# Attention, routed experts and a feed-forward layer on one core: drains on POOL, attention's tiles in two pools, weight conversions at other times

## The chip, the cores and the metric

The kernel runs on one core of a Trainium2 chip. The metric is device time in microseconds of one execution; it was 872.88 us in the median of three runs (872.65 to 874.85). One execution was also profiled. The core's engines work side by side, each through its own instructions in order: TensorE (PE), VectorE (DVE), ScalarE (ACT), GpSimd (POOL) and SyncE (SP, which here issues most DMAs).

## The reference

Three layers follow each other; all is float32 except the last layer's weights, which come as float64 (the kernel reads them as pairs of 32-bit words).

```python
# attention: batch 4, heads 8, sequence 576, head 64
scores = q @ k.T / sqrt(64);  cum = cumsum(maximum(s, 0))
scores = where(causal, -1e9, scores + minimum(-(cum[..., :, None] - cum[..., None, :]), 0))
x = softmax(scores) @ v                      # -> 2304 tokens of 512
# experts: 8 of 512 -> 1024 -> 512, one for each token
e_idx = argmax(x @ w_gate)
out[mask_e] = gate_w * eom_e * (maximum(x[mask_e] @ w1[e], 0) @ w2[e])
# feed-forward: 512 -> 2048 -> 512
y = square(maximum(out @ w_in, 0)) @ w_out
```

## The kernel before

Attention goes over 16 pairs of heads and ends near 224 us. Its tiles lie in a stack of pools that is closed after it; the pools of the later stages are then opened on the same addresses. The first of them, `stg`, holds three staging buffers of 4 KB a partition; `wpool2` with the weight slots w2 and w3 (32 KB each) follows.

The expert stage has 64 units. Unit n = 8 g + f handles slice f (128 hidden features) of expert g, for all tokens of that expert at once (352 token rows for the first, less for the later ones; the first 128 of expert 0 are computed earlier). Its work is H (`emit_h`, L1426, twelve matmuls of xt and w into PSUM), a split of the rectified result into a high and a low part (`emit_hv`: ACT writes the high part at L1436, DVE the low part at L1437), and Y (`emit_y`, L1468, twelve matmuls: the first eight read the high part, the last four the low part). The operands are float32r tiles, and each value is held as a high part and the rest; weights are split alike: `w_load` (L237) brings 512 KB into a staging buffer from SP's queue, `w_hi` (L246) writes the high part on ACT, `w_lo` (L250) the low part on DVE. Eight such jobs make an expert's weights.

The order on each engine is written by hand. `at(key, function)` files a piece of work under a key, counted in units; all pieces are emitted in the order of their keys, and where two keys are equal in the order of filing. An engine's queue is then worked through in that order: a piece that waits holds up what was filed behind it on the same engine. H of unit n has key n, its split n + 0.9, its Y n + 2.1, so Y runs behind H of two units later. The four PSUM sums of an expert are copied out by `emit_yv` on ACT (L1515, key 9.5 after the expert's start) and must be free before the next expert's first Y.

```python
at(n, emit_h, g, g, f, f)
at(n + K_['hv'], emit_hv, g, f)
at(n + 2.1, emit_y, g, g, f, f, NF)
```

Among these units sixteen pieces of the feed-forward weights are converted from float64 to float32 in DRAM, one in K_['cvp'] units from key K_['cv0'] on. A piece is loaded at K_['cvl'] = 2.5 units before its key (L1366; the first two from ACT's queue, the others from SP's), worked on by ACT (L1378, L1382) and DVE (L1376 to L1390), put together on POOL (`cv_c`, L1394 and L1395) in a single buffer cvm, and stored from ACT's queue (L1400, key + 2.4); the next piece's L1382 waits for that store to land. The other sixteen pieces are converted in the feed-forward stage.

Before unit 0, the first 128 tokens of expert 0 go through `early_h` (L1069) and `early_y` (L1097), which read hidden values from the tile `st_a[1]` of attention; `early_store` (key 0.5, L1584 to L1587) writes their result.

The feed-forward stage works on six tiles of 384 tokens; each tile's result is stored by `y_store` (L1536) with three indirect DMAs from POOL, which puts the rows at their tokens' places. After the last tile comes a loop for overflowing experts that runs zero times here, and the program's closing instructions, which the profile puts down to L1813.

Of the kernel before, what the change touches and what calls it, by code (L numbers as in the profile page):

```python
# [13 lines left out]
F32R = mybir.dt.float32r  # L14
# [10 lines left out]
P = 128  # L25
# [5 lines left out]
    S=3,  # L31
# [42 lines left out]
    exs=5.6,  # L74
    exl=8.6,
    cvm=0.7,
    cvp=3.5,
    cv0=4.0,
    cvl=2.5,
    ws=0.75,  # L80
    wh=0.3,
# [9 lines left out]
def attention_moe_ffn_kernel(  # L91
# [14 lines left out]
    nc = tc.nc  # L106
    B, H, S, D = q.shape
    NT, DM = out.shape
    E = w_gate.shape[1]
# [14 lines left out]
    NTILE = NT // TT  # L124
# [92 lines left out]
    def at(key, fn, *args):  # L217
        tasks.append((key, len(tasks), fn, args))
# [33 lines left out]
    def w_job(job, t_load, t_hi, t_lo):  # L252
        if job not in raw:
            at(t_load, w_load, job)
        at(t_hi, w_hi, job)
        at(t_lo, w_lo, job)
# [18 lines left out]
    def half_jobs(e, ab):  # L275
        return [((e, ab), i) for i in range(4)]
# [4 lines left out]
    def rows_of(g):  # L281
        if g >= E:
            return [P] * CT
        return [P] * (CAPS[g] // P) + ([CAPS[g] % P] if CAPS[g] % P else [])
# [4 lines left out]
    def cols_of(g):  # L289
        return sum(rows_of(g)) - P * first_of(g)  # L290
# [159 lines left out]

    with tc.manual_schedule():
        with ExitStack() as actx:
            apool = actx.enter_context(tc.tile_pool(name="apool", bufs=1))
            cq_p = actx.enter_context(tc.tile_pool(name="cq", bufs=1))
            qk_p = actx.enter_context(tc.tile_pool(name="qk", bufs=3))
# [9 lines left out]
            p2ctx = ExitStack()  # L465
            ps_2 = p2ctx.enter_context(tc.tile_pool(name="ps_2", bufs=1, space=PSUM, side="right"))

            st_a = [apool.tile([P, 4, S], F32R, name=f"sta{a}") for a in range(3)]
            st_b = [apool.tile([P, 4, S], F32R, name=f"stb{a}") for a in range(2)]

            def st_of(pp):
                return st_a[pp % 3], st_b[pp % 2]
# [873 lines left out]
        def x_trans(g, c, t, d=0.0):  # L1346
            at(t, x_pe, g, c)
            at(t + d + 0.001, x_hi, g, c)
            at(t + 2 * d + 0.002, x_lo, g, c)
# [177 lines left out]
        def y_store(g):  # L1527
            ysb = ysb_t.pop(g)
            if g < E:
                n = cols_of(g)  # L1530
                dst = yT_d.rearrange("(k p) n -> p k n", p=P)
                nc.sync.dma_start(
                    out=dst[:, :, P:P + n] if g == 0 else dst[:, :, ds(reg_o[g], n)], in_=ysb[:, :, 0:n])
                return
            for c in range(CT):
                put = nc.gpsimd.indirect_dma_start(  # L1536
                    out=out[:, :], out_offset=bass.IndirectOffsetOnAxis(ap=tok_m[:, (g - E) * CT + c, 0:1], axis=0),
                    in_=ysb.rearrange("p a n -> p (a n)")[:, c * DM:(c + 1) * DM], in_offset=None)
                nc.gpsimd.memset(gap, 0.0)
                for old in puts:  # L1540
                    tc.declare_no_dep(put.ins, old.ins, reason="the rows of two sorted chunks are different tokens")
                puts.append(put)

        def pos_tokens():
            w = gt2("pz", [B * NB, E])
            nc.vector.tensor_tensor(
                out=w, in0=oh_all.rearrange("p b t e -> p (b t) e"),
                in1=R["v"][:, 1:2].to_broadcast([P, B * NB, E]), op=ALU.mult)
            x = gt2("py", [B * NB])
            nc.vector.tensor_reduce(out=x.unsqueeze(2), in_=w, axis=AX.X, op=ALU.add)  # L1550
            nc.vector.tensor_tensor(
                out=pos_i.rearrange("p b t -> p (b t)"), in0=x, in1=rk_all.rearrange("p b t -> p (b t)"), op=ALU.add)
            nc.vector.tensor_copy(out=tok[:, :, :, 1].bitcast(F32), in_=gsq)
# [49 lines left out]
        for n in range(NS):  # L1603
            g, f = divmod(n, NF)
# [3 lines left out]
        for g in range(E):  # L1608
            n0 = g * NF
            if g:  # L1610
                at(n0 + NF + 1.0, load_regs, [g], 1, reg_o, NT)
            if g > 1:
                at(n0 - NF - 1.5, load_regs, [g], 0, reg_e, E - 1)
            at(n0 + NF + 1.5, emit_yv, g)
            at(n0 + NF + 1.8, y_store, g)
            if g + 1 < E:
                for c in range(len(rows_of(g + 1))):
                    x_trans(g + 1, c, n0 + K_['xt0'] + K_['xt1'] * c if g else 4.2 + 1.0 * c, 0.3)
            if g + 2 < E:
                at(n0 + (6.7 if g == 0 else 5.5), gather, g + 2)  # L1620
            hj = half_jobs(g + 1, "a") + half_jobs(g + 1, "b")
            at(n0 + 2.15, alloc_next)
            at(n0 + 2.15, alloc_next)
            for i, job in enumerate(hj):
                ta = n0 + 2.2 + i
                if g + 1 == E and i >= 6:
                    continue
                w_job(job, -0.7 if g == 0 and i < 4 else ta - K_["wld"], ta + K_['wh'], ta + K_['wl'])
# [34 lines left out]
        for v, (t, f0, f1) in enumerate(visits):  # L1663
            g = E + t
            if v > 1 and not (f0 and t not in spilled):
                n0 = n - 6 if v == 2 else n - 7.5
                at(n0 - 4.0, load_xf, t)
                for i in range(2):
                    ks = (i * KD // 2, (i + 1) * KD // 2)
                    at(n - 5.04 + 2 * i, xf_hi, t, *ks)  # L1670
                    at(n - 5.04 + 2 * i, xf_lo, t, *ks)
            for f in range(f0, f1):
                e = E + f // NF
                at(n, emit_h, g, e, f, f % NF)
                at(n + 0.9, emit_sq, g, f)
                at(n + 0.94, emit_hs, g, f)
                left = NTILE * NF2 - 1 - n
                if left == 0:
                    at(n + 2.1, emit_y_end, g, e, [f - 1, f], NF2)
                elif t in spilled:  # L1680
                    at(n + 2.1, emit_y, g, e, f, f % NF, f1, f0)
                elif left > 1:
                    at(n + 2.1, emit_y, g, e, f, f % NF, NF2)
                n += 1
            if f1 == NF and t in spilled:
                for c in range(CT):
                    at(n + 1.97 + c, emit_ym, g, c)
            elif f1 == NF2:
                at(n + 1.2, emit_ys if t in spilled else emit_yv, g)
                at(n + 1.8, y_store, g)  # L1690
# [15 lines left out]
        else:  # L1706
            for i, job in enumerate(half_jobs(E + 1, "a") + half_jobs(E + 1, "b")):
                ta = 3.5 + 3.0 * i
# [108 lines left out]
```

## Time and profile before

| | us |
|---|---|
| median of three runs | 872.88 |
| the runs | 872.65, 872.88, 874.85 |
| the profiled execution | 871.05 |
| its span, first to last instruction | 869.3 |
| PE, DVE, ACT, POOL busy in it | 843.5, 519.9, 452.1, 261.4 |

The stages of the profiled execution: attention until about 224 us, the early part of expert 0 until 238.7, the 64 units until about 459, the feed-forward layer until 856, and closing instructions until 869.3. PE's rows give the start of matmuls that run on into one another; their lengths overlap, so the time of a group of twelve is read from its start to the next group's start. In brackets stands the idle time of the engine just before a row, and what ended it. Rows of a queue ("ACTq", "SPq") are instructions of its sequencer, such as the issue of a DMA; they do not count as busy.

### The profile page before, as it was taken

The numbers are of one execution on the slowest core, as the hardware profiler recorded it, in microseconds if no ns is written. First come the engines' busy times: TensorE is split into PE (matmuls) and PEld (weight loads), VectorE is DVE, ScalarE is ACT, GpSimd is POOL, SyncE is SP. The second block draws the span as 40 slices with busy tenths as digits, with TensorE's granted clock in tenths as the row PEclk, the third lists the DMA queues.
The fourth block names the chain that finished last, engine by engine and source line by source line (L and its number), as shares of the span: only waits on it lengthen the run. The fifth ranks groups of instructions, "written<-read, shape, count | busy, mean of one in ns | idle before, by whom it ended". The sixth has DMA issues, their size and how long they took to land.

```text
span 869.3 us, 15155 instructions
## 1 busy us (share of the span) xinstructions
PE 843.5 (97%) x5412; PEld 748.8 (86%) x5412; DVE 519.9 (60%) x1186; ACT 452.1 (52%) x1008; POOL 261.4 (30%) x302
## 2 busy tenths in 40 slices
PE   7999999999999999999999999999999999999993
PEld 5876777777789999999999999999999999999992
DVE  8667777978768587668866667664333333232220
ACT  6687878988446556566555555443323232223221
POOL 4322234543136575566412233331101101001001
PEclk9999999999999999999999999999999999999998
DMA  6666677753178898899883442321010111001001
GB/s 155 147 157 145 142 181 179 176 130 94 42 268 250 271 266 244 241 272 284 291 241 98 134 135 84 109 85 49 37 37 37 59 51 37 1 1 37 1 1 39
DMA packets 113028, 113.14 MB, mean 130 GB/s; under 512 B 66033, under 2 KB 83953, under 8 KB 112946
## 3 DMA queue, kind: packets, MB, share of 16 engines
q1 hardware_dynamic: 106162, 96.97, 40.9%
q0 software_dynamic: 3664, 9.62, 3.2%
q10 hardware_dynamic: 3120, 5.51, 1.8%
q8 instruction: 45, 0.74, 0.4%
q14 instruction: 37, 0.30, 0.1%
HBM read 80.50 MB, written 23.32 MB: 119 GB/s over the span
## 4 chain that ended last, share of the span: by engine, by line
PE 52%; issue 30%; ACT 5%; DVE 4%; DMA 4%; POOL 3%; SPq 0%; POOLq 0%; ACTq 0%; DVEq 0%
PE z L1426 17%; PE z L1468 10%; PE z L1477 7%; PE t L731 5%; PE s L634 4%; PE t L694 4%; ACT p L678 2%; POOL out_dram L1536 2%; DMA w_out_d<-cvm 1%; DMA cv<-in_moe_w_in_dram 1%; ACT sta L574 1%; PE t L547 1%; ACT pt L713 1%; PE z L333 1%; PE s L769 1%
## 5 line engine op out<-in xcount | busy, mean ns | idle before, releaser
L1426 PE MATMUL z<-xt,w 128*128 128x384 f32 (+6 forms) x1920 | 329.9, 320 | 1.9 <-DVE h L1437 1.9
L1426 PEld LDWEIGHTS z<-xt,w 128*128 128x128 f32 x1920 | 308.3, 188 | 10.8 <-DVE h L1437 2.1
L1477 PE MATMUL z<-w,h 128*128 128x512 f32 x864 | 214.9, 393 | 0.0
L1477 PEld LDWEIGHTS z<-w,h 128*128 128x128 f32 x864 | 160.8, 188 | 29.3
L1446 DVE SCALAR_TENSOR_TENSOR r<-z,r 128x384 f32<-128x384 f32 x96 | 53.3, 555 | 129.1 <-ACT r L1445 127.5
L1445 ACT ACTIVATE r<-z 128x384 f32<-128x384 f32 x96 | 47.2, 491 | 153.5 <-PE z L1426 150.6
L1468 PE MATMUL z<-h,w 128*128 128x304 f32 (+5 forms) x768 | 112.1, 295 | 0.1
L1468 PEld LDWEIGHTS z<-h,w 128*128 128x128 f32 x768 | 105.3, 191 | 0.6 <-ACT ysb L1515 0.3
L1394 POOL TENSOR_TENSOR cvm<-cvm,cva 128x512 f32<-128x512 f32 x32 | 47.2, 1475 | 182.6 <-DVE cva L1390 135.5
L1536 POOL DMA_INDIRECT out_dram<-ysb,tok_m x18 | 17.4, 969 | 245.5 <-ACT ysb L1523 183.2
L1453 DVE TENSOR_TENSOR h<-r,h 128x384 fp32r<-128x384 f32 x96 | 60.9, 635 | 50.3 <-ACT h L1452 47.4
L678 ACT ACTIVATE p<-p,nm 128x128 f32<-128x128 f32 (+3 forms) x144 | 84.3, 590 | 4.8 <-DVE nm L661 4.7
L1452 ACT CAST h<-r 128x384 fp32r<-128x384 f32 x96 | 49.3, 513 | 63.6 <-DVE r L1446 63.2
L661 DVE CUSTOM_DVE_ANT_0 p<-s,mask 128x128 f32<-128x128 f32 (+3 forms) x128 | 59.5, 485 | 29.1 <-PE s L634 28.0
L694 PE MATMUL t<-ident,p 128*128 128x128 f32 x400 | 69.5, 283 | 2.6 <-DVE sta L578 1.1
L250 DVE TENSOR_TENSOR w<-stg,w 128x1024 fp32r<-128x1024 f32 x49 | 68.7, 1401 | 0.8 <-ACT w L246 0.8
L246 ACT CAST w<-stg 128x1024 fp32r<-128x1024 f32 x49 | 51.5, 1051 | 20.3 <-POOL cvm L1395 19.4
L694 PEld LDWEIGHTS t<-ident,p 128*128 128x128 f32 x400 | 44.4, 140 | 18.8 <-ACT p L678 6.8
L595 POOL CAST stb<-sta 64x1152 fp32r<-64x1152 f32 x28 | 31.4, 1150 | 79.3 <-PE s L634 47.7
L1395 POOL TENSOR_TENSOR cvm<-cvs,cvm 128x512 f32<-128x512 f32 x32 | 54.0, 1688 | 2.5
L634 PE MATMUL s<-sta 128*64 128x288 f32 (+4 forms) x204 | 50.1, 342 | 3.3 <-ACT sta L574 1.2
L1437 DVE SCALAR_TENSOR_TENSOR h<-z,h 128x304 fp32r<-128x304 f32 (+5 forms) x64 | 28.5, 445 | 40.8 <-ACT h L1436 33.9
(242 smaller groups left out, 1041.6 us busy)
## 6 DMA issues: line engine op xcount, KB each, us to landing
stg<-in_moe_w_dram SPq DMA_DIRECT2D x42, 512.0 KB
cv<-in_moe_w_out_dram SPq DMA_DIRECT2D x16, 512.0 KB
stx<-in_moe_w_dram SPq DMA_DIRECT2D x14, 512.0 KB
cv<-in_moe_w_in_dram SPq DMA_DIRECT2D x14, 512.0 KB
xr<-yT_d SPq DMA_DIRECT2D x8, 768.0 KB
qk<-in_q_dram SPq DMA_DIRECT2D x32, 128.0 KB
qk<-in_k_dram SPq DMA_DIRECT2D x32, 128.0 KB
v<-in_v_dram SPq DMA_DIRECT2D x32, 128.0 KB
```

The costliest lines, as they stand in the source:

```text
L246: nc.scalar.copy(out=w_parts(job)[0], in_=raw[job])
L250: nc.vector.tensor_tensor(out=lo, in0=raw.pop(job), in1=hi.bitcast(F32), op=ALU.subtract)
L634: nc.tensor.matmul(ps[0:mw, d0:d0 + nn], lhsT=ql[r, m0:m0 + mw], rhs=kl[r, c0:c0 + nn], start=(i == 0 and (tail or n == 0)), stop=(done an ...
L661: nc.vector.tensor_tensor_reduce(out=dst, in0=src, in1=msk, scale=-1.0, scalar=3.0e38, op0=ALU.add, op1=ALU.min, accum_out=nm[:, c:c + 1])
L678: nc.scalar.activation(out=pt[:, cs], in_=pt[:, cs], func=AF.Exp, scale=-1.0, bias=nm[:, c:c + 1], accum_out=rs[:, r:r + 1])
L694: nc.tensor.transpose(tp[:, i * P:(i + 1) * P], pt[:, j0:j0 + P], ident)
L1395: nc.gpsimd.tensor_tensor(out=m, in0=sq, in1=m, op=ALU.add)
L1426: nc.tensor.matmul(ps[:, 0:n], lhsT=wa[:, zw, kk, fl * P:(fl + 1) * P], rhs=xt[:, zx, kk, 0:n], start=(i == 0), stop=(i == 3 * KD - 1))
L1446: nc.vector.scalar_tensor_tensor(out=gg, in0=ps[:, 0:TT], scalar=0.0, in1=gg, op0=ALU.max, op1=ALU.mult)
L1453: nc.vector.tensor_tensor(out=ht[:, 1], in0=gg, in1=ht[:, 0].bitcast(F32), op=ALU.subtract)
L1468: nc.tensor.matmul(y_acc[g][d][:, 0:n], lhsT=wb[:, zw, fl, d * P:(d + 1) * P], rhs=ht[:, zh, 0:n], start=(f == 0 and i == 0), stop=(f == n ...
L1477: nc.tensor.matmul(acc, lhsT=ht[:, zh, c * P:(c + 1) * P], rhs=wb[:, zw, fl, :], start=(first and i == 0), stop=(last and i == 2))
```

## The change

Four things change. In the feed-forward stage a `drain` is put on POOL behind the stores of every tile but the last. Attention's tiles `st_a[0]` and `st_b[0]` come from a pool of their own that lies ahead of the pool with all others. Expert 1's weights are allocated from key 0.1 and converted with keys 0.2 + 1.2 i (high part + 0.3, low part + 0.7) in place of 2.2 + i; the loads of jobs 4 to 7 keep their lead of 2.9. The feed-forward weights are converted from key 6.0 on, one in 3.4 units, in place of 4.0 and 3.5.

```diff
-    cvp=3.5,
-    cv0=4.0,
+    cvp=3.4,
+    cv0=6.0,
...
+            apool0 = actx.enter_context(tc.tile_pool(name="apool0", bufs=1))
             apool = actx.enter_context(tc.tile_pool(name="apool", bufs=1))
...
-            st_a = [apool.tile([P, 4, S], F32R, name=f"sta{a}") for a in range(3)]
-            st_b = [apool.tile([P, 4, S], F32R, name=f"stb{a}") for a in range(2)]
+            st_a = [(apool if a else apool0).tile([P, 4, S], F32R, name=f"sta{a}") for a in range(3)]
+            st_b = [(apool if a else apool0).tile([P, 4, S], F32R, name=f"stb{a}") for a in range(2)]
...
                 puts.append(put)
+            if g + 1 < E + NTILE:
+                nc.gpsimd.drain()
...
-            at(n0 + 2.15, alloc_next)
-            at(n0 + 2.15, alloc_next)
+            at(n0 + 2.15 if g else 0.1, alloc_next)
+            at(n0 + 2.15 if g else 0.1, alloc_next)
             for i, job in enumerate(hj):
-                ta = n0 + 2.2 + i
+                ta = n0 + 2.2 + i if g else 0.2 + 1.2 * i
...
                 w_job(job, -0.7 if g == 0 and i < 4 else ta - K_["wld"], ta + K_['wh'], ta + K_['wl'])
```

## Rows read from the trace of the kernel before

**Rows 1.** The page, part 1: busy us (share of the span) xinstructions.
```profile
PE 843.5 (97%) x5412; PEld 748.8 (86%) x5412; DVE 519.9 (60%) x1186; ACT 452.1 (52%) x1008; POOL 261.4 (30%) x302
```

**Rows 2.** Windows: length, busy of PE, PEld, DVE, ACT, POOL, clock, DMA share, GB/s.
```profile
253.00:256.50 3.50, 1.62 (x15) 1.39 (x14) 3.36 (x6) 3.50 (x7) 1.63 (x2) 1.00 0.55 162
256.50:260.00 3.50, 3.50 (x18) 3.30 (x18) 3.36 (x10) 1.19 (x2) 1.79 (x1) 0.51 0.44 120
```

**Rows 3.** Timeline, PE: start, duration, engine, line, op, names, shape, [idle before, releaser].
```profile
243.15 1.50 PE L1468 MATMUL z<-h,w 128*128 128x224 f32 x12
244.49 1.50 PE L1426 MATMUL z<-xt,w 128*128 128x224 f32 x12
...
255.44 1.94 PE L1426 MATMUL z<-xt,w 128*128 128x224 f32 x12 [1.88 <-DVE h L1437]
257.18 2.76 PE L1468 MATMUL z<-h,w 128*128 128x224 f32 x12
259.87 0.47 PE L333 MATMUL z<-ident,xr 64*128 64x64 f32 x4
```

**Rows 4.** Timeline of ACT and its queue, 241 to 253 us.
```profile
241.77 0.36 ACT L1436 ACTIVATE h<-z 128x224 fp32r<-128x224 f32 x1 [0.51 <-ACT ysb L1586]
241.79 0.50 ACTq L1366 DMA_DIRECT2D cv<-in_moe_w_in_dram  x1
...
242.59 1.04 ACT L246 CAST w<-stg 128x1024 fp32r<-128x1024 f32 x1
...
252.04 0.69 ACT L1378 ACTIVATE cvs<-cv 128x512 f32<-128x512 f32 x1 [5.29 <-DMA cv<-in_moe_w_in_dram]
```

**Rows 5.** Timeline of DVE, 242 to 253 us.
```profile
242.16 0.39 DVE L1437 SCALAR_TENSOR_TENSOR h<-z,h 128x224 fp32r<-128x224 f32 x1 [1.71 <-ACT ysb L1586]
...
245.30 1.22 DVE L250 TENSOR_TENSOR w<-stg,w 128x1024 fp32r<-128x1024 f32 x1
...
252.04 0.43 DVE L1376 TENSOR_SCALAR cva<-cv 128x512 int32<-128x512 int32 x1 [3.03 <-DMA cv<-in_moe_w_in_dram]
```

**Rows 6.** Waits of SP's queue, 200 to 300 us: total, times, longest.
```profile
SPq L237 <- PE z L1097: 3.2, 1, 3.2
```

**Rows 7.** Timeline of SP's queue near 239 us.
```profile
239.02 1.46 SPq L237 DMA_DIRECT2D stg<-in_moe_w_dram  x3
```

**Rows 8.** Timeline of ACT and its queue, 427 to 440 us.
```profile
427.21 0.33 ACTq L1400 DMA_DIRECT2D w_out_d<-cvm  x1
...
433.25 0.69 ACT L1382 ACTIVATE cvm<-cv 128x512 f32<-128x512 uint16 x1 [1.15 <-DMA w_out_d<-cvm]
433.83 1.23 ACT L1515 COPY ysb<-z 128x272 f32<-128x272 f32 x4
...
439.28 0.33 ACTq L1400 DMA_DIRECT2D w_out_d<-cvm  x1
```

**Rows 9.** Timeline of PE, H of units 57, 58 and 59.
```profile
429.60 1.59 PE L1426 MATMUL z<-xt,w 128*128 128x256 f32 x12
...
432.54 1.58 PE L1426 MATMUL z<-xt,w 128*128 128x256 f32 x12
...
436.29 1.60 PE L1426 MATMUL z<-xt,w 128*128 128x256 f32 x12
```

**Rows 10.** Line L1813: durations in ns (min/median/max), first and last start.
```profile
L1813 POOLq DRAIN  x3: 51/103/5048, 863.4 to 869.0; - x3
```

**Rows 11.** Line L1802, the program's start, the same columns.
```profile
L1802 POOLq DRAIN  x1: 187/187/187, 0.4 to 0.4; - x1
```

**Rows 12.** Timeline of POOL, 852 to 870 us.
```profile
853.78 0.95 POOL L1536 DMA_INDIRECT out_dram<-ysb,tok_m  x1 [57.75 <-ACT ysb L1523]
```

**Rows 13.** DMA issues of POOL's queue, the three largest groups.
```profile
xr<-x_d,tbl_p POOLq DMA_INDIRECT x20
tok_d<-tok,pos_i POOLq DMA_INDIRECT x20
...
out_dram<-ysb,tok_m POOLq DMA_INDIRECT x18
```

## Prediction

> **What bounds the kernel now.** I began with the page's busy shares: TensorE's matmuls cover 97% of the span [rows 1], so only a stretch in which PE waits or runs at its low clock, or one in which nothing is computed, can give time back. I then read the windows and PE's timeline, looking for such stretches. There are three that this diff reaches.
>
> The first lies in unit 5 to 6 of the expert stage (a unit is one slice of 128 hidden features: twelve matmuls of L1426, H, and twelve of L1468, Y). An undisturbed group of twelve takes 244.49 - 243.15 = 1.34 us. Then PE idles for 1.88 us until DVE has finished a hidden slice (L1437), the next H takes 257.18 - 255.44 = 1.74 us and the next Y 259.87 - 257.18 = 2.69 us [rows 3]. The granted clock was 1.00 in the stretch that holds the idle time and 0.51 in the one after it, so the second loss is the 1.2 GHz level behind the first [rows 2]. Why the slice was late is seen on the in-order queues: the first load of FFN weights was issued from ACT at 241.79, and ACT (5.29 us) and DVE (3.03 us) both stood until 252.04 with that conversion at their heads [rows 4, 5]. Loss: 1.88 + 0.40 + 1.35 = 3.6 us.
>
> The second is small: H of unit 57 to H of unit 58 takes 432.54 - 429.60 = 2.94 us, the next one 436.29 - 432.54 = 3.75 us [rows 9], because ACT waited 1.15 us for a weight store to land before it could copy expert 6's sums out of PSUM (L1382 at 433.25, then L1515 at 433.83) [rows 8]. Loss: 0.8 us.
>
> The third is the tail. The last row stores start at 853.78 [rows 12], and among the closing instructions POOL has one DRAIN of 5.05 us, the first of its three, at 863.4 [rows 10]. It ends at 868.4, in a span of 869.3.
>
> **FFN conversion from unit 6 on.** The load moves from key 1.5 to 3.5, the conversion from 4.0 to 6.0, so the distance stays 2.5 units. Undisturbed that is 2.5 x 2 x 1.34 = 6.7 us, less than the 10.25 us that the load took now. What shortens it is what it competes with: at 241.79 it was issued right behind four loads of expert 1 that had left from 239.02 on [rows 7]; from key 3.5 it is issued after those have mostly landed. I place the issue at 245.6 and ACT's need for it at 254.5 (hidden slice 5 and two transposes stand ahead of it), 8.9 us apart. If the load still took 10.25 us, ACT would wait 1.3 us, a quarter of today's 5.29 us, and Y runs two units behind its slice, which hides that. So all 3.6 us go. The ends: 0 if the wait only moves, 3.6 if it goes.
>
> **Expert 1's conversion from unit 0.5.** Eight high parts on ACT (1.04 us each, row at 242.59) and eight low parts on DVE (1.22 us, row at 245.30) are the same work as before, spread over 1.2 units each and begun two units earlier. What is new is who stands behind the first. Its high part gets key 0.5 and goes ahead of hidden slice 0 on ACT, at about 241.77, where slice 0 starts now. Its low part gets key 0.2 + 0.7, which is 0.8999 in floating point, and so goes ahead of slice 0 (0.9) on DVE as well. Slice 0 is then ready on ACT at 241.77 + 1.04 + 0.36 = 243.17, just when PE wants it (243.15), but on DVE only at 242.85 + 1.22 + 0.39 = 244.46, in place of 242.16 + 0.39 = 242.55 [rows 3 to 5]. Y reads the high parts for its first eight matmuls and the low part from the ninth on, that is from 243.15 + 8 x 0.11 = 244.05. PE waits 0.4 us there. I take 0.4; the ends are 0 (Y only starts later in a queue that catches up) and 1.9, the longest PE wait in the trace [rows 3]. Later high parts stand at most one slice ahead of a hidden slice that Y needs two units later, which hides them; without that cover each would cost its 1.04 us.
>
> **Two pools.** The first weight load now waits 3.2 us for the last L1097 matmul [rows 6], which reads an attention tile at the place where the staging buffers come to lie. Of the tiles put into the first pool none is used by that early expert work, so the loads should leave 3.2 us earlier, near 235.8 instead of 239.02 [rows 7]. This is not on PE's path; it is what lets the first two conversions find their data. I take 0 for it; if it fails, conversions wanted at 241.8 and 243.0 wait for data instead, at most those 3.2 us, and PE loses part of what step one gains. Weight slot w2 itself still waits for L1097, which ended by 239.02, and its first conversion comes at 241.8: no cost.
>
> **Period 3.4.** The last conversions do not fit their period: store to store takes 439.28 - 427.21 = 12.07 us [rows 8], while 3.4 units of 2.94 us are 10.0. Starting two units later they end half a unit later (57.0 in place of 56.5), so ACT's waits for landed stores grow. On the other side the order at the boundary turns: the wait of conversion 15 gets key 57.7 and stands behind the copy at 57.5, where it was ahead with 57.2. So today's 0.8 us goes; but stores with keys 25.4 and 49.2, for which ACT waits on POOL, now stand just ahead of the copies at 25.5 and 49.5. I take a gain of 0.4; ends: gain 0.8, loss 1.6 (two such boundaries).
>
> **Five drains on POOL.** They follow the stores of five of the six token tiles. POOL has nothing to do there: it idles 57.75 us before the last store [rows 12], and the weight conversions are over by then, so even five drains of 5 us each are hidden. The question is what they leave for the last one. A drain costs 0.187 us at the program's start, when POOL has done nothing [rows 11], and 5.048 us at the end, when it has issued 58 indirect DMAs by the three largest groups [rows 13]. The last one starts after the output's DMAs were awaited, so it is not waiting for these. If its time is bookkeeping of what has gathered since the previous drain, three DMAs are left of 58: 5.05 x 3 / 58 = 0.26. Bounds: gain 0 if the time does not depend on a backlog, 4.86 if it falls to 0.187. I take 4.8, because the cheap row is the only one with no DMA before it.
>
> **Sum.** 3.6 - 0.4 + 0 + 0.4 + 4.8 = 8.4 us. The profiled run took 871.05 us, 1.75 outside its span of 869.3; that gives 862.65. The median of the runs shown is 872.88, 0.2% above the profiled run, and the same subtraction gives 864.5 us.
>
> **Rivals.** (a) The last drain does not shrink, because its time belongs to ending the program or to the last three DMAs. For it: just one long drain is on record, so nothing shows that it scales. Against it: POOL's other two closing drains are 0.05 to 0.1 us [rows 10], so closing as such is cheap. Only the expert stage gains: 872.88 - 3.6 = 869.3 us. The Trainium skill ("VectorE: DVE Perf Modes", The DRAIN you can't avoid) counts the drains of a program's frame as a constant of about 12 ns on every engine, by which five more would change nothing and the sum would be that of this rival; POOL's 5048 ns does not agree with it.
>
> (b) The drain shrinks, but the wait in the expert stage only moves to units 6 to 8 and keeps its price: 872.88 - 4.8 = 868.1 us. For it: same 2.5 units of lead.
>
> (c) Neither comes: the loads still leave at 239.02, ACT waits as long at another head, the drain stays. 872.9 us.
>
> (d) Slower: from about unit 40 the conversion's round through ACT, POOL and the landed store takes over as the bound, since it needs 12.07 us for a period of 10.0. Seven conversions (9 to 15) gather 7 x 2.07 = 14.5 us of lateness; one unit, 2.9 us, is hidden by the order of H and Y; the other 11.6 reach PE where ACT's waits hold the slices. Against the gains of 3.6 - 0.4 + 4.8 = 8.0 that is 3.6 us more than now: 876.5 us. It decides when ACT is over a unit late at the copy of key 49.5. Against it: the same round was longer than 3.5 units already, and cost 0.8 us in all.
>
> **Chances.** Forecast 0.54, (a) 0.28, (b) 0.06, (c) 0.07, (d) 0.05. The forecast's own range is 862 to 867; with most of (a) and (b) it is 862.0 to 870.3. A measurement of this kernel can tell 0.3% (2.6 us) from no change. Below 870.3 lie the forecast, (b) and nine tenths of (a): faster 0.85; same 0.10; slower 0.05.
>
> **What would show it.** Right: the first expert load leaves near 236; ACT's and DVE's waits for the first FFN-weight load are under 1.5 us; PE has no idle second between 245 and 265 and keeps clock 1.00 there; one wait near 244 of about 0.4 us, in the middle of the first Y; the last POOL drain under 0.5 us, the first one in the FFN some 4 us. Wrong: a closing drain of still 5 us (then (a)), a half-clock window near 247 (the first Y waited longer than worked out), or L1515 starting later than half a unit after its key.

## The result and the profile after

The changed kernel takes 862.60 us in the median of four runs (861.85 to 867.50), the kernel before 872.76 on the same chip (four runs, 871.69 to 874.85): ratio 0.9899, 95% interval [0.9871, 0.9926]. The profiled execution took 862.62 us, its span is 860.9. Against the profiled execution of before that is 8.4 us less, in the medians it is 10.2; the section on the drains alone says where the other 1.8 probably come from.

The page's first part for the changed kernel. PE's work is what it was [rows 1]; the span around it is shorter, so its share rises by a point.

```profile
PE 841.9 (98%) x5412; PEld 747.3 (87%) x5412; DVE 523.8 (61%) x1186; ACT 450.7 (52%) x1008; POOL 260.0 (30%) x302
```

The windows that answer to [rows 2]. PE is busy through both, and the granted clock stays at 1.00 where it was 0.51, that is at 2.4 GHz in place of 1.2.

```profile
253.00:256.50 3.50, 3.50 (x34) 3.50 (x33) 2.95 (x12) 2.17 (x5) 0.00 (x0) 1.00 0.35 125
256.50:260.00 3.50, 3.50 (x33) 3.32 (x32) 3.33 (x8) 2.79 (x6) 1.85 (x2) 1.00 0.62 192
```

PE's timeline, three stretches that answer to [rows 3] and [rows 9]. The lines of the new kernel are one to three higher: H is L1427 here, Y L1469.

```profile
243.57 1.13 PE L1469 MATMUL z<-h,w 128*128 128x224 f32 x8
244.89 0.70 PE L1469 MATMUL z<-h,w 128*128 128x224 f32 x4 [0.19 <-DVE h L1438]
245.43 1.50 PE L1427 MATMUL z<-xt,w 128*128 128x224 f32 x12
...
254.26 1.58 PE L1427 MATMUL z<-xt,w 128*128 128x224 f32 x12
255.68 1.50 PE L1469 MATMUL z<-h,w 128*128 128x224 f32 x12
...
427.57 1.59 PE L1427 MATMUL z<-xt,w 128*128 128x256 f32 x12
...
430.50 1.59 PE L1427 MATMUL z<-xt,w 128*128 128x256 f32 x12
...
433.37 1.60 PE L1427 MATMUL z<-xt,w 128*128 128x256 f32 x12
```

Three things are to be seen. The first Y breaks after its eighth matmul and waits for DVE's low part: it takes 245.43 - 243.57 = 1.86 us where an undisturbed group takes 1.34, so 0.52 are lost. The stall near 255 is gone: from H at 254.26 to Y at 255.68 is 1.42 us, with no idle time noted. And H of unit 57 to 58 to 59 is now 2.93 and 2.87 us, where the second was 3.75.

Why, on the queues. ACT's timeline first (the load of the FFN weights is the ACTq row), then DVE's, then SP's queue; they answer to [rows 4, 5 and 7].

```profile
242.19 1.05 ACT L246 CAST w<-stg 128x1024 fp32r<-128x1024 f32 x1 [0.51 <-ACT ysb L1589]
243.15 0.35 ACT L1437 ACTIVATE h<-z 128x224 fp32r<-128x224 f32 x1
...
243.78 0.36 ACTq L1367 DMA_DIRECT2D cv<-in_moe_w_in_dram  x1
...
255.28 0.68 ACT L1379 ACTIVATE cvs<-cv 128x512 f32<-128x512 f32 x1
```

```profile
243.27 1.26 DVE L250 TENSOR_TENSOR w<-stg,w 128x1024 fp32r<-128x1024 f32 x1 [2.39 <-ACT w L246]
244.46 0.67 DVE L1438 SCALAR_TENSOR_TENSOR h<-z,h 128x224 fp32r<-128x224 f32 x2
```

```profile
235.55 1.48 SPq L237 DMA_DIRECT2D stg<-in_moe_w_dram  x3
```

The FFN weights' load has 255.28 - 243.78 = 11.5 us, and ACT takes it up without a wait (no bracket), where it stood 5.29 us. On DVE the early weight split of 1.26 us stands ahead of the hidden slice: that is the 0.52 us in the first Y. The expert's loads leave 3.47 us earlier.

ACT is not rid of waiting, though. POOL now gathers expert 2's tokens (three L303 DMAs, 257.84 to 262.64) ahead of putting the first weight piece together, and ACT's queue stands until it can store that piece. POOL's last step, then ACT and its queue:

```profile
264.25 1.29 POOL L1396 TENSOR_TENSOR cvm<-cvs,cvm 128x512 f32<-128x512 f32 x1
```

```profile
265.57 0.33 ACTq L1401 DMA_DIRECT2D w_in_d<-cvm  x1
266.00 0.44 ACT L1437 ACTIVATE h<-z 128x320 fp32r<-128x320 f32 x1 [6.00 <-PE z L1469]
...
267.85 1.08 ACT L1516 COPY ysb<-z 128x224 f32<-128x224 f32 x4
```

ACT idles 6.00 us here, where before the change it stood 2.05 us for the same store, besides the 5.29 for the load. The bracket names PE; in the kernel with the conversion alone (below) the same wait, 5.65 us, is put down to POOL's step. PE feels little of it: H of unit 10 to 11, with expert 1's first Y between them, takes 4.28 us, 3.89 before.

The end of the program: POOL's DRAINs in the FFN (L1545), the closing ones (L1816, as [rows 10]) and INC_SWDGE_SEM, an instruction on the same queue that the profile puts down to the loop for overflowing experts (L1722); durations are min/median/max in ns.

```profile
L1545 POOLq DRAIN  x5: 3023/3271/5074, 624.5 to 791.9; - x5
...
L1816 POOLq DRAIN  x3: 51/103/292, 859.6 to 860.6; - x3
...
L1722 POOLq INC_SWDGE_SEM  x1: 240/240/240, 857.9 to 857.9; - x1
```

The same instruction before the change:

```profile
L1719 POOLq INC_SWDGE_SEM  x1: 1404/1404/1404, 860.6 to 860.6; - x1
```

The closing DRAIN falls from 5.048 to 0.292 us. The INC_SWDGE_SEM falls too, by 1.16 us, which no step had. The five drains that pay for it take 3.0 to 5.1 us each (the first 5.07, where some 4 were forecast) and cost PE nothing: from the FFN's first H to the last matmul it is 402.97 us in both kernels.

The span in five parts, divided by the starts of four matmuls (H of unit 0, H of unit 8, the FFN's first H, and the last one): 238.71, 263.06, 452.13 and 855.10 us before, 239.13, 260.27, 449.21 and 852.18 after.

| | before | after | less by | forecast |
|---|---|---|---|---|
| start to H of unit 0 | 238.71 | 239.13 | -0.42 | 0 |
| H of unit 0 to H of unit 8 | 24.35 | 21.14 | 3.21 | 3.6 - 0.4 |
| H of unit 8 to first H of the FFN | 189.07 | 188.93 | 0.14 | 0.4 |
| FFN, first H to last matmul | 402.97 | 402.97 | 0 | 0 |
| last matmul to end | 14.20 | 8.74 | 5.46 | 4.8 |

The sum is 8.4 us. Of the 0.14, 0.88 are won at unit 58 and 0.39 each lost at units 10 and 27. H of unit 0 starts anywhere from 238.6 to 241.5 in the profiles of all kernels below, without a pattern by kernel.

### The profile page after: what moved, and what is told of

The parts are those of the page before. It is cut to its first block, busy times and chain, and to the rows that moved or that the text cites. A ratio compares the mean times of both kernels' runs of the same rounds, so it can differ in the third digit from the quotient of the medians.

```text
span 860.9 us, 15163 instructions
## 1 busy us (share of the span) xinstructions
PE 841.9 (98%) x5412; PEld 747.3 (87%) x5412; DVE 523.8 (61%) x1186; ACT 450.7 (52%) x1008; POOL 260.0 (30%) x302
## 4 chain that ended last, share of the span: by engine, by line
PE 56%; issue 30%; ACT 5%; DVE 4%; POOL 2%; DMA 1%; POOLq 1%; SPq 1%; ACTq 0%; DVEq 0%
PE z L1427 19%; PE z L1469 11%; PE z L1478 7%; PE t L732 5%; PE s L635 5%; PE t L695 4%; ACT p L679 2%; POOL out_dram L1537 1%; ACT sta L575 1%; PE z L333 1%; PE t L548 1%; ACT pt L714 1%; PE s L770 1%; POOLq L1545 1%; PE t L827 1%
## 5 line engine op out<-in xcount | busy, mean ns | idle before, releaser
L1427 PE MATMUL z<-xt,w 128*128 128x384 f32 (+6 forms) x1920 | 329.6, 320 | 0.1
L1427 PEld LDWEIGHTS z<-xt,w 128*128 128x128 f32 x1920 | 308.1, 188 | 9.0 <-DVE h L1438 0.4
L1469 PE MATMUL z<-h,w 128*128 128x304 f32 (+5 forms) x768 | 111.0, 293 | 0.2 <-DVE h L1438 0.2
L1469 PEld LDWEIGHTS z<-h,w 128*128 128x128 f32 x768 | 104.0, 189 | 0.6 <-DVE h L1438 0.4
L1395 POOL TENSOR_TENSOR cvm<-cvm,cva 128x512 f32<-128x512 f32 x32 | 44.2, 1381 | 168.1 <-DVE cva L1391 128.3
L250 DVE TENSOR_TENSOR w<-stg,w 128x1024 fp32r<-128x1024 f32 x49 | 73.6, 1502 | 5.4 <-ACT w L246 5.4
L714 ACT COPY pt<-t 128x512 f32<-128x512 f32 (+1 forms) x94 | 47.0, 515 | 7.3 <-PE t L732 4.1
```

Of the source, the lines that this page charges most:

```text
L250: nc.vector.tensor_tensor(out=lo, in0=raw.pop(job), in1=hi.bitcast(F32), op=ALU.subtract)
L714: nc.scalar.copy(out=dst, in_=src)
L1427: nc.tensor.matmul(ps[:, 0:n], lhsT=wa[:, zw, kk, fl * P:(fl + 1) * P], rhs=xt[:, zx, kk, 0:n], start=(i == 0), stop=(i == 3 * KD - 1))
L1469: nc.tensor.matmul(y_acc[g][d][:, 0:n], lhsT=wb[:, zw, fl, d * P:(d + 1) * P], rhs=ht[:, zh, 0:n], start=(f == 0 and i == 0), stop=(f == n ...
```

## Experiments

### The drains alone, and all but the drains

```diff
 # drains_only: the kernel before, with
                 puts.append(put)
+            if g + 1 < E + NTILE:
+                nc.gpsimd.drain()
 # no_drains: the changed kernel, without these two lines
```

> The kernel before with the five POOL drains and nothing else. Backlog theory (a drain's time is bookkeeping of the indirect DMAs issued since the drain before it): the closing drain is 0.3 us as in the changed kernel (5.05 before), the last wait of POOL's queue ahead of it is 0.24 us in place of 1.40, the wait in the expert stage near 253 us stays; 4.8 to 6 us less than before, about 867.5. Rival (the tail got short because of something in the expert stage, for instance other positions of the instructions): the closing drain stays near 5 us and the time within 1 us of before.

> The changed kernel without its drains. My theory: the two parts add. The closing drain is 5.05 us again, H of unit 8 starts 21.1 us after H of unit 0 (24.35 before), PE's last matmul is some 3 us earlier than before: about 869.5. Rival (the drains also help inside the feed-forward stage): more than 1.5 us of the gain that is not in the tail goes with them, over 871.

Measured: the drains alone 867.56 us (six runs; before 872.95), ratio 0.9932 [0.9907, 0.9957]; all but the drains 869.64 us (ten runs), 0.9970 [0.9951, 0.9989]. The two gains, 0.68% and 0.30%, add up to 0.98%; both together had given 1.01%. PE's last matmul, expected 3 us earlier without the drains, came only 0.45 earlier in the profile (854.65), since H of unit 0 started 2.4 us later there. The rows of the two closings (the drains alone, then all but the drains):

```profile
L1815 POOLq DRAIN  x3: 51/103/292, 865.8 to 867.5; - x3
...
L1721 POOLq INC_SWDGE_SEM  x1: 240/240/240, 864.1 to 864.1; - x1
```

```profile
L1814 POOLq DRAIN  x3: 51/103/5048, 862.8 to 868.4; - x3
```

These rows save 4.76 + 1.16 = 5.9 us, and 0.68% of 873 is 5.9, with an interval of 3.7 to 8.1. From the last matmul to the end it is 14.0 to 14.4 us in the three profiles without a drain and 8.7 to 9.7 in the nine with a drain behind the fifth tile, 5.1 less on the means. So rival (a), a closing drain that stays as it is, falls. In the kernel with the drains alone the stall is still there, and longer than in the profile of before. Its PE timeline:

```profile
255.21 0.60 PE L333 MATMUL z<-ident,xr 128*128 128x128 f32 x4
259.62 2.43 PE L1426 MATMUL z<-xt,w 128*128 128x224 f32 x12 [3.82 <-DVE h L1437]
```

PE idles 3.82 us, against 1.88 [rows 3]. H of unit 0 to unit 8 took 24.35, 26.34, 25.83 and 26.76 us in the four profiles with the old keys (before, the drains alone, and the two kernels of the next section), and 21.13 or 21.14 in the five profiles of the changed kernel, of it without some or all drains, and of it with another period. So the new keys of the two conversions were worth 3.2 to 5.6 us there, and the profiled execution of before was the one with the shortest stall of the four. That probably makes the 1.8 us by which the medians differ more than the profiles; it isn't shown, since the other executions of before were not profiled and start H of unit 0 at times of their own.

### What the closing drain counts

```diff
 # drain_early: the kernel before, with one drain in the expert stage
         at(NS - 3.4, get_tokens)
+        at(5.0, nc.gpsimd.drain)
 # drain_mid: the kernel before, with one drain in the FFN
         at(0.6, xf_hi, 1)
+        at(36.0, nc.gpsimd.drain)
 # drain_last_but_one: the changed kernel, with the last of the five only
-            if g + 1 < E + NTILE:
+            if g == E + NTILE - 2:
                 nc.gpsimd.drain()
```

> The kernel before with one drain on POOL at key 5.0 of the expert stage, where POOL has issued 6 of its 61 indirect DMAs, and none later. Backlog of DMAs (0.05 us + 0.082 us for each DMA since the drain before, a line through 3 DMAs: 0.29 us and 61: 5.05 us): this drain 0.5 us, the closing one (55 DMAs) 4.55 us. Rival one-time cost (the first drain after some DMA pays it, for instance to bring in its code): this drain about 5 us, the closing one 0.3 us. Rival backlog of all POOL instructions (302 for 5.05 us, some 160 of them after key 5): closing drain 2.7 us.

> The kernel before with one drain on POOL at key 36 of the feed-forward stage, behind the last weight conversion and ahead of the first row store: 43 DMAs before it, 18 after it. Backlog of DMAs: this drain 3.6 us, the closing one 1.5 us. Rival one-time cost: about 5 us and 0.3 us. Rival backlog of all POOL instructions (some 37 left): closing drain 0.6 us.

> The changed kernel with one drain only, behind the stores of the fifth of the six tiles. Backlog theory: that drain takes 58 x 0.082 = 4.8 us once its DMAs are issued, hidden in 57 us of idle POOL, and the closing one 0.3 us: same time as the changed kernel. Rival (each of the five drains takes its part away for good and one is not enough): closing drain over 1 us.

The closing drains and increments of the three, in this order:

```profile
L1814 POOLq DRAIN  x3: 51/103/4543, 864.1 to 869.2; - x3
...
L1720 POOLq INC_SWDGE_SEM  x1: 1280/1280/1280, 861.4 to 861.4; - x1
```

```profile
L1814 POOLq DRAIN  x3: 51/103/1522, 866.0 to 868.1; - x3
...
L1720 POOLq INC_SWDGE_SEM  x1: 540/540/540, 864.1 to 864.1; - x1
```

```profile
L1816 POOLq DRAIN  x3: 51/103/297, 860.6 to 861.9; - x3
```

| indirect DMAs of POOL since the last drain | closing drain, us | INC_SWDGE_SEM, us |
|---|---|---|
| 61 (before) | 5.048 | 1.404 |
| 55 | 4.543 | 1.280 |
| 18 | 1.522 | 0.540 |
| 3 (changed kernel) | 0.292 | 0.240 |

Both are straight lines: (5.048 - 0.292) / 58 = 0.082 us for each DMA plus 0.05 for the drain, 0.020 us for each plus 0.18 for the increment; 55 and 18 DMAs fall on them to 0.01 us. A price paid once, which any first drain would take away, would have given a small closing drain after the early one too; it gave 4.543. Counted in rows in place of DMAs (6992 rows in the 61, 2304 in the 18, 384 in the 3), a line through the last two would give 4.5 us for the first, not 5.048.

The two drains inside the programs took longer than expected: 2.757 us at key 5.0 (0.5 expected, six DMAs) and 4.924 in the FFN (3.6 expected, 43). Each row begins while POOL still works on the addition ahead of it (L1395, until 259.72 and 595.74); counted from there they take 0.59 and 3.59 us, against 0.54 and 3.58 on the line.

One drain behind the fifth tile does as much for the closing as five: 0.297. The kernel with it takes 864.15 us (four runs; before 874.29), 0.9888 [0.9866, 0.9911]; its drain takes 6.235 us and stands where POOL idles. The two other kernels ran once, at 871.18 and 870.16 us.

### The conversion from unit 6 alone

```diff
-    cvp=3.5,
-    cv0=4.0,
+    cvp=3.4,
+    cv0=6.0,
```

> The kernel before with cv0=6.0 and cvp=3.4 alone; expert 1's weights as before. My theory: the load that ACT and DVE stood for was just called too early, so moving it takes all 3.6 us away; no 0.5 us wait at the first Y, H of unit 8 about 20.7 us after H of unit 0; 869.2. Rival (expert 1's earlier conversion is needed to empty the DMA queues first): the load, called at key 3.5 behind weight loads that still leave at 239, lands over 9 us later, ACT stands 2 us or more for it and PE gets back less than 2 us.

Measured: 868.16 us (eight runs; before 872.95), ratio 0.9939 [0.9919, 0.9959]. H of unit 0 to unit 8 is 20.63 us, so this edit alone removes the stall, with the expert's loads still near 239.7 and one pool. PE's timeline of its first Y:

```profile
243.79 1.50 PE L1468 MATMUL z<-h,w 128*128 128x224 f32 x12
245.13 1.50 PE L1426 MATMUL z<-xt,w 128*128 128x224 f32 x12
```

The group takes 1.34 us undisturbed, so the 0.5 us of the changed kernel belong to expert 1's early conversion. But H of unit 8 to the FFN takes 191.31 us in its profile, against 188.2 to 189.4 in the four with the old keys: some 2.5 us lost further on. That was the first sign against my 0.4 us of gain for this part. The time does not bear the 2.5 out: the edit gains 3.6 to 7.1 us by its interval, while the stall of the four profiles (on the mean 5.2 us longer than here) less 2.5 is 2.7, and the profiled execution, 870.37, was the second slowest of its eight.

### The hidden slice ahead of the early conversion

```diff
-                ta = n0 + 2.2 + i if g else 0.2 + 1.2 * i
+                ta = n0 + 2.2 + i if g else 0.65 + 1.2 * i
```

> The changed kernel with expert 1's keys 0.65 + 1.2 i in place of 0.2 + 1.2 i, so that the split of hidden slice 0 (0.9) goes ahead of the first high part (0.95) on ACT and of the first low part (1.35) on DVE. My theory: the first Y takes 1.34 us in place of 1.86, everything else stays: 0.5 us less than the changed kernel in the span. Rival (the slice waits for something else): the first Y stays at 1.8 us or more, or the later conversions put a wait before unit 10 that costs as much.

Measured: 865.11 us (four runs; before 872.95), ratio 0.9907 [0.9871, 0.9942]. The first Y is mended (H of unit 0 to unit 8: 20.62 us), yet there is no gain: H of unit 8 to the FFN takes 192.67. Two of the new waits, in PE's timeline, and ACT's copy that the first is for:

```profile
268.29 2.33 PE L1469 MATMUL z<-h,w 128*128 128x320 f32 x12 [0.82 <-ACT ysb L1516]
...
274.41 0.60 PE L333 MATMUL z<-ident,xr 128*128 128x128 f32 x4
275.80 1.43 PE L1427 MATMUL z<-xt,w 128*128 128x320 f32 x8 [0.79 <-DVE h L1438]
```

```profile
267.91 1.07 ACT L1516 COPY ysb<-z 128x224 f32<-128x224 f32 x4
```

The second half of the rival comes true, if at unit 10 and not before it. The copy of expert 0's sums starts at 267.91, in the changed kernel at 267.85: behind the store of the first weight piece (265.63 and 265.57) it stays where it was, and what PE won at the first Y it waits for here. With the second wait, H of unit 10 to 12 takes 10.27 us in place of 8.23.

### One pool for attention's tiles

```diff
-            apool0 = actx.enter_context(tc.tile_pool(name="apool0", bufs=1))
...
-            st_a = [(apool if a else apool0).tile([P, 4, S], F32R, name=f"sta{a}") for a in range(3)]
+            st_a = [apool.tile([P, 4, S], F32R, name=f"sta{a}") for a in range(3)]
```

(`st_b` likewise; all else as in the changed kernel.)

> The changed kernel with attention's tiles in one pool again. My theory: the first weight loads leave near 239 in place of 235.6, and the conversions called at 242.2 and 243.4 find data that lands only then: ACT waits up to 3 us for them with hidden slices 0 and 1 behind it, and PE loses 1 to 3 us of the 3.2 us that the stage gained, perhaps with the low clock after it. Rival (the early loads are not needed): H of unit 8 still 21.1 us after H of unit 0, same time.

Measured: 863.86 us (four runs; before 874.29), ratio 0.9884 [0.9862, 0.9907]. SP's queue, ACT and PE of this kernel:

```profile
238.91 0.93 SPq L237 DMA_DIRECT2D stg<-in_moe_w_dram  x2
```

```profile
242.67 1.05 ACT L246 CAST w<-stg 128x1024 fp32r<-128x1024 f32 x1 [1.52 <-DMA stg<-in_moe_w_dram]
...
245.13 1.05 ACT L246 CAST w<-stg 128x1024 fp32r<-128x1024 f32 x1 [1.16 <-DMA stg<-in_moe_w_dram]
```

```profile
244.02 1.15 PE L1468 MATMUL z<-h,w 128*128 128x224 f32 x8 [0.83 <-issue]
```

Without the second pool the loads leave 3.4 us later, the early conversions wait for their data, and PE stands 0.83 us ahead of its first Y: H of unit 0 to unit 8 is 22.13 us, 1.0 more than with two pools. So the second pool does what it was said to do for the early conversion; the later conversion alone needs none, and no run has the second pool without the early conversion. In this profile H of unit 8 to the FFN takes 191.75 us, against 188.9 to 190.6 with two pools. The time shows neither loss, as the rival had it; the profiled execution was the slowest of the four.

### Two parts, the period, and the changed kernel beside them

```diff
 # two_parts: the kernel before, with
+            if g + 1 < E + NTILE:
+                nc.gpsimd.drain()
...
-    cvp=3.5,
-    cv0=4.0,
+    cvp=3.4,
+    cv0=6.0,
 # two_parts_35: the same, but cvp stays 3.5
 # period_35: the changed kernel, but cvp stays 3.5
 # after_again: the changed kernel
```

> The kernel before with two of the four parts: the five drains, and the FFN conversion from unit 6 with period 3.4. Expert 1 is converted from unit 2.2 as before, and attention's tiles stay in one pool. Theory: these two carry the whole gain. Measured alone they gave 0.9932 and 0.9939; both together 0.987, that is some 861.9 us where the kernel before takes 873.3; H of unit 0 to H of unit 8 20.6 us (no wait in the first Y, 0.5 less than with all four parts), closing drain 0.29. So not slower than the changed kernel, and up to 1 us faster. Rival: the early conversion of expert 1 and the second pool are what keeps the later units on time: with them H of unit 8 to the FFN took 188.9 to 190.6, with the conversion alone 191.3. Then this kernel stands at 191.3 again, and is 1 to 2 us slower than the changed kernel.

> As the kernel with two parts, but with the period of 3.5 units that the kernel before has; the last piece then has key 58.5 in place of 57.0. Theory (the period is what costs a microsecond late): a round of conversion took 12.07 us against 10.0 us in 3.4 units and 10.3 in 3.5; the five extra microseconds over sixteen pieces take most of the late waits away: H of unit 8 to the FFN 189 in place of 191, time 1 to 2 us under the kernel with period 3.4. Rival (order): the late waits come from which store wait stands ahead of which PSUM copy; another period only draws other pairs: 190 to 192, and no difference that can be told.

> The changed kernel with period 3.5 in place of 3.4, nothing else. Theory (the period costs a microsecond): H of unit 8 to the FFN under 189.0, time 0.5 to 1.5 us less than the changed kernel beside it. Rival (order): 189 to 191 and the same time. By the step of the prediction that gave the period a gain of 0.4: 0.4 us slower, since the wait of 0.8 us at the copy of expert 6 comes back.

> The changed kernel itself, to stand beside the other three on one chip. Expected: ratio to the kernel before 0.988 to 0.990; H of unit 0 to H of unit 8 21.1 us, H of unit 8 to the FFN 188.9 to 190.6 us, closing drain 0.29 us.

| | median us (runs) | ratio to before (873.09) | H of unit 0 to 8 | H of unit 8 to FFN |
|---|---|---|---|---|
| drains, conversion from 6, period 3.4 | 863.67 (4) | 0.9898 [0.9858, 0.9938] | 20.62 | 191.12 |
| the same, period 3.5 | 863.88 (5) | 0.9900 [0.9869, 0.9931] | 20.62 | 190.54 |
| changed kernel, period 3.5 | 863.11 (4) | 0.9894 [0.9854, 0.9934] | 21.13 | 188.65 |
| changed kernel | 862.78 (4) | 0.9886 [0.9846, 0.9927] | 21.13 | 188.94 |

PE's rows for two of these stretches in the kernel with two parts (H of unit 0, of unit 8, and the first of the FFN):

```profile
241.45 0.26 PE L1426 MATMUL z<-xt,w 128*128 128x224 f32 x1
...
262.08 0.32 PE L1426 MATMUL z<-xt,w 128*128 128x320 f32 x1
...
453.20 0.34 PE L1426 MATMUL z<-xt,w 128*128 128x384 f32 x1
```

262.08 - 241.45 = 20.6 and 453.20 - 262.08 = 191.1; in the changed kernel the same three starts are 239.13, 260.27 and 449.21. So two of the four parts carry nearly the whole gain: the drains and the later start. In the time the period does nothing that can be measured, with or without the rest, and the theory that it costs a microsecond is not borne out. The traces show where it costs. Here is PE, H of units 27 and 28, before and then in the changed kernel:

```profile
330.26 1.92 PE L1426 MATMUL z<-xt,w 128*128 128x304 f32 x12
...
334.03 1.22 PE L1426 MATMUL z<-xt,w 128*128 128x304 f32 x7
```

```profile
327.86 1.92 PE L1427 MATMUL z<-xt,w 128*128 128x304 f32 x12
...
332.02 1.24 PE L1427 MATMUL z<-xt,w 128*128 128x304 f32 x7
```

This step takes 4.15 to 4.30 us in all eight profiles with period 3.4 and 3.76 in all six with 3.5: in the changed kernel DVE works off four conversion steps between two hidden slices (327.03 and 331.50), and the weight load of H waits 0.39 us for the second. H of unit 51 to 52 is 0.4 to 0.7 us longer in four of the eight. The 0.8 us at the copy of expert 6 are another matter. In the kernel with the drains alone, ACT has the same order as in [rows 8] and no wait:

```profile
435.91 0.68 ACT L1382 ACTIVATE cvm<-cv 128x512 f32<-128x512 uint16 x1
436.48 1.24 ACT L1515 COPY ysb<-z 128x272 f32<-128x272 f32 x4
```

H of unit 58 to 59 takes 2.87 us there and with the early drain, 3.75 and 3.68 in the other two with the old keys, 3.56 with one pool and 3.92 in the second kernel of the table. The loss comes and goes with the old keys, and also comes with new ones.

The rival of the first of these expectations has the traces for it and not the times. With the early conversion and the second pool, H of unit 8 to the FFN took 188.93, 189.47, 190.59 and 188.94 us (the changed kernel, it without drains, with one drain, and again; mean 189.5), without them 191.31 and 191.12. But four profiles of one and the same expert stage differ by 1.7 us, and the 191.12 comes from an execution of 867.19 us where the other three took 863.3 to 863.9. The times differ by 0.9 us in that direction, and their intervals overlap. No version here beats the changed kernel.

## Why the prediction was right, point by point

The forecast of 864.5 us was 1.9 too high, within its range. The forecast for the profiled pair, 8.4 us, came out at 8.4. Four of the five steps were right; that the sum fits so well is luck, since the tail gave 0.7 more than its 4.8, and the start of H and the later units 0.4 and 0.3 less than forecast.

- **The conversion from unit 6** ("all 3.6 us go"): shown. ACT's wait for the load is gone: the load had 11.5 us and not the 8.9 worked out, since it was issued at 243.78, 1.8 earlier than placed, and needed at 255.28, 0.8 later. The conversion alone, with 8.8 us (246.18 to 254.97), does without a wait too, so the load took less there than the 10.25 of before. What the step did not see is the 6.00 us that ACT then waits for POOL in units 8 and 9, of which at most 0.4 reach PE at unit 10. The stall's size was taken from one execution; against the conversion alone it was 3.7 us there and up to 6.1 in others, which probably made the median forecast too high.
- **Expert 1 from unit 0.5** ("PE waits 0.4 us"): shown at the place forecast, behind the eighth matmul of the first Y, with 0.52. The kernel with the slice ahead of the conversion shows that the order of the two makes it: there the wait is gone.
- **Two pools** ("I take 0"): the loads leave at 235.55, forecast 235.8. Undone, they cost 1.0 us of the 3.2 given as the bound, at the two conversions named, and nothing that the time shows.
- **Period 3.4** ("I take a gain of 0.4"): this step failed. The 0.8 us at the copy of expert 6 did go in the pair, but they are also absent from two of the four profiles with the old period, so the new order there can't be given the credit. The loss feared at the boundaries of experts 3 and 6 did come near the first, 0.4 us at unit 27 in every profile with period 3.4, though for a hidden slice on DVE and not for a store ahead of a copy, and near the second, at unit 51, in four of the eight. And the later start lengthens the later units where the step had no term: with it alone they took 191.3 us in the profiles, 191.1 with the drains, against a mean of 188.7. The early conversion with the second pool, costed at nothing there, has 189.5 on the mean. So the pair's gain of 0.14 is the luck of two executions; on the means it would be a loss of 0.8, and the times can tell neither.
- **Five drains** ("4.8"): 4.76. The division 5.05 x 3 / 58 gave 0.26, measured 0.292; the count that belongs there is 61 DMAs, and 0.05 us do not scale. The increment's 1.16 us were missed, though its row was in the trace: I looked at the longest instruction of the tail and not at what else stood on its queue there.

Of the rivals, (a) falls by the drain rows. The Trainium skill's rule beside it ("VectorE: DVE Perf Modes", The DRAIN you can't avoid), by which a frame's drains are a constant of about 12 ns on all engines, does not hold for POOL here: 0.29 to 5.05 us. (b) had the move right and the price wrong: ACT's wait went to units 8 and 9, but eight units take 21.14 us and the granted clock is 1.00 at 253 to 260. (c) falls with these and the drain. (d), the conversion's round as the bound, has something for it in the late waits, such as those at unit 51, but not its price of 11.6 us: in the worst profile with period 3.4 the units from 8 on are 4.0 us longer than on the mean before. Why so little of the conversion's lateness reaches PE no run here shows.

What stays open: what share of 188.7 to 192.7 us in the later units belongs to a kernel and what to the single execution, since each kernel but the changed one was profiled once. Some causes are found (the copy behind the first store at unit 10, DVE's conversion steps at unit 27); for the others, at units 18, 43, 51 and 61, I did not find the pair of instructions.

## What to carry to other kernels

Where a program issues indirect DMAs from POOL, look at POOL's closing DRAIN in the trace: where it grows with their number, as here, one drain where POOL idles anyway, behind the last but one group of stores, takes it off the end. Where an engine in order stands for a transfer, the work that needs the transfer can be filed later; but here each shift of such work brought waits further on, so read the whole stage and not only the stall, and undo the parts one by one before a gain is put down to one of them. And when a stall comes from a race between a load and its use, take its size from several executions.

## What the runs showed of the hardware

- POOL's closing DRAIN costs 0.082 us for each indirect DMA since the previous drain, and the INC_SWDGE_SEM 0.020 us for each, over 3 to 61 of them. I had expected the first by an argument and the second not at all. A drain's row can begin before the operation ahead of it has ended; counted from that end, two drains with no DMA of POOL under way took 0.59 and 3.59 us and fit the same line.
- A drain behind stores that are under way also waits for them. The second one of the FFN starts at 657.91, before the last store's row has begun (658.05), and ends at 660.93, 1.9 us after that row's end at 659.02; the stores' landing is put at 2.7 us after issue. For the backlog of three DMAs alone the line above gives 0.3 us. The Trainium skill says of this ("Perfetto Trace Analysis", DMA Instruction — SWDGE (GPSIMD)) that such a row ends when the descriptors are made and not when the data has moved; the drain's later end agrees. What those 3 us cost an engine with work in its queue was not measured.
- The stall in the expert stage had another length in each of four profiles (24.35 to 26.76 us for eight units), while the same eight units without it came out within 0.01 us of each other in five.
